# Which engine transposes blocks 10 to 23: the DMA crossbar or TensorE

## The chip, the cores and the metric

The kernel runs on one core of a Trainium2 chip. The metric is the device time of one execution in microseconds; for the kernel before there are three runs, and their median counts.

## The reference

Attention with a sliding window and four sink positions, for 4 batches of 8 heads, 768 positions and head size 64, followed by a normalised MLP with a residual:

```python
scores = scale * np.matmul(q, k.transpose(0, 1, 3, 2))
keep = (pos[None, :] < 4) | ((rel >= 0) & (rel < 128))      # rel = row - column
a = softmax(np.where(keep, scores, -1e9))
attn = a @ v                                                # x: heads side by side, (4, 768, 512)
xn = (x - mean) / sqrt(var + 1e-6) * g_ln
out = x + np.maximum(xn @ w_ch1, 0.0) @ w_ch2               # w_ch1 512x2048, w_ch2 2048x512
```

## The kernel before

The rows are cut into 24 blocks of 128 (6 for each batch). Block t needs its own q, k and v and the k and v of block t - 1, and from the third block of a batch on also the four sink positions. For each block the kernel does the following.

- *Load* (L265 to L285): q, k and v come from HBM as bf16 into `qkn` and `vn`, by DMAs that POOL issues. `qkn` lives in the ring `ld` of four buffers.
- *Transpose of q and k* into `qkT` (ring `qk`, five buffers). Blocks 0 to 9 use TensorE: eight 128x128 transposes at L348 into one PSUM bank `pt`, and a copy at L354 from there, by ACT or DVE. Blocks 10 to 23 use one DMA transpose at L370, issued by SP, from `qkn` straight to `qkT`. Either way the transpose gives the `ld` buffer back.
- *Scores* at L407 (`ps`), sink scores at L414 (`pk`, with `ks`, the sink keys of the batch copied at L455 from the batch's first `qkT`), exponentials on ACT at L436 and L483 (`e`, `es`), the mask on DVE at L445.
- *Values* at L497, L502 and L505 (`po`), normalisation on DVE at L515 and L518 (`xt`), the centred and scaled row `xc` at L530, and the variance at L539 and L540.
- *Transpose of `xc`* into `xnt`, the MLP's input for a group of four blocks. Blocks 0 to 9: four TensorE transposes at L561 into a bank `px`, and a copy at L576 by ACT or DVE. Blocks 10 to 23: one DMA transpose at L567, issued by SP.

The MLP works on six groups of four blocks. `m1` has 16 quanta of four 128x512 matmuls (L599, `ph`), each followed by a ReLU on ACT or DVE (L612 or L610, `h`); `m2` has 16 quanta of four (L625, `pc`), and after every fourth DVE adds the residual, scaled with `rsg` (L637, `ot`), and SP stores a block (L644). That is 192 quanta. `rsg` is made on POOL at L550.

The order on every engine is written when the program is built. `Planner` takes each piece of work as a task with estimated costs, the buffers that it takes and gives back, and a priority; it repeatedly takes the task that could start earliest by its estimates, so attention and MLP quanta are interleaved on TensorE. On the chip each engine works through its list in that order and waits where an input or a buffer is not there yet. The scores of block t from t = 5 on depend on quantum 8(t - 4) - 8 (the last loop of the kernel), which spreads them over the MLP. Four PSUM banks, the ring `pa`, serve `pt`, `px`, `po`, `pk`, `pv`, `ph` and `pc`; two double banks serve `ps`. In the first 24 us `warm` fills planned gaps of TensorE with matmuls that nobody reads (L184).

The two branches that test the set `DTR` are these:

```python
elif t in DTR:          # L363
    def dtr(e, s): ...  # one dma_start_transpose for all of q and k, on SP
...
if t in DTR:            # L563
    def dxt(e, *s2): ...  # one dma_start_transpose of xc, on SP
```

Of the kernel before, what the change touches and what calls it, by code (L numbers as in the profile page):

```python
# [129 lines left out]
def kernel(  # L130
# [22 lines left out]
    NT = B * RB  # L153
# [177 lines left out]
    def block(t):  # L331
# [27 lines left out]
        if split:  # L359
# [6 lines left out]
            d_t[t] = tq  # L366
        elif t in DTR:
            def dtr(e, s):
                qkT[t] = buf("qk", s, [128, 2, 4, 128], BF16, "qkT")
                nc.sync.dma_start_transpose(qkT[t].rearrange("p a h c -> p (a h) c"),  # L370
                                            qn[t].rearrange("p a h d -> p (a h d)"))
# [190 lines left out]

        if t in DTR:  # L563
            def dxt(e, *s2):
                if s2:
                    xnt[g] = buf("xn", s2[0], [128, NDM, 512], BF16, "xnt")
                nc.sync.dma_start_transpose(xnt[g][:, :, 128 * ti:128 * (ti + 1)], xc[t])  # L567
# [79 lines left out]

    SPLIT = set(range(8))
    SPLIT_S = set(range(4))
    DTR = set(range(10, NT))  # L650
    DTL = 1.5
    LAND = .9
    WARM_UNTIL = 24.0
# [62 lines left out]
```

## Time and profile before

| what | value |
|---|---|
| median of three runs | 231.85 us (231.32 to 232.07) |
| profiled execution: time | 232.07 us |
| profiled execution: span | 230.3 us |
| TensorE busy | 222.6 us, 97% |
| VectorE busy | 135.3 us, 59% |
| ScalarE busy | 106.6 us, 46% |
| GpSimd busy | 76.2 us, 33% |
| granted TensorE clock | 0.998 of full speed |
| `qkT<-qkn` DMA transposes | 14, landing after 7.6 us (median) |
| `xnt<-xc` DMA transposes | 14, landing after 3.4 us (median) |

The span runs from the first to the last instruction of the profiled execution; its time is 1.8 us more, for what lies around the span. In the profile PE is TensorE, PEld its weight loads, DVE VectorE, ACT ScalarE, POOL GpSimd and SP the queue engine; a tile `out<-in` names what is written and read, and L is the line of the kernel. The busy share of an engine is an average over stages; the chain of waits is followed back from the last instruction to what released each step. A matmul's length contains the depth of the pipeline, so lengths of neighbouring matmuls overlap, and their cost is the distance from one start to the next.

### The profile page before, as it was taken

How to read it: one execution, taken by the hardware profiler on the slowest of the kernel's cores; microseconds unless marked ns; L12 is line 12 of the kernel's file. 1: busy time of each engine (PE TensorE's matmuls, PEld its weight loads, DVE VectorE, ACT ScalarE, POOL GpSimd, SP SyncE). 2: the span in 40 equal slices, each digit the busy share in tenths (PEclk: the TensorE clock that was granted, in tenths of full speed). 3: DMA queues.
4: the chain of work that ended last, by engine and by line, in shares of the span. 5: the costliest groups of instructions: out<-in, count | busy, mean ns of one | idle time of the engine just before them, and what ended most of it. 6: DMA issues, size and time to landing. Idle time of an engine off the chain costs nothing.

```text
span 230.3 us, 4775 instructions
## 1 busy us (share of the span) xinstructions
PE 222.6 (97%) x1950; PEld 118.3 (51%) x1950; DVE 135.3 (59%) x376; ACT 106.6 (46%) x162; POOL 76.2 (33%) x92
## 2 busy tenths in 40 slices
PE   8999998999999999999999999999999999999993
PEld 7567543566555555444545544454554554444441
DVE  5775800399998959765567666845855755100121
ACT  2387266568456751156650356642067530276000
POOL 7993174988435780734041400001000001000000
PEclk9999999999999999999999999999999999999999
DMA  7999999999999999996959982023121022200112
GB/s 46 141 157 204 201 206 168 155 182 157 140 174 128 160 164 154 191 173 118 109 36 179 150 181 54 16 55 117 54 62 23 0 55 85 91 0 3 46 46 91
DMA packets 104983, 25.74 MB, mean 112 GB/s; under 512 B 97793, under 2 KB 101889, under 8 KB 104962
## 3 DMA queue, kind: packets, MB, share of 16 engines
q0 software_dynamic: 79104, 13.64, 80.9%
q1 hardware_dynamic: 25858, 11.80, 26.2%
q8 instruction: 15, 0.25, 0.4%
q14 instruction: 6, 0.05, 0.1%
HBM read 27.27 MB, written 6.29 MB: 146 GB/s over the span
## 4 chain that ended last, share of the span: by engine, by line
PE 77%; DMA 15%; POOL 5%; DVE 1%; issue 1%; ACT 0%; POOLq 0%
PE pc L625 36%; PE ph L599 28%; DMA qkn<-in_k_dram 7%; PE ps L407 4%; DMA w1s<-in_moe_w_ch_dram 4%; DMA qkT<-qkn 3%; PE po L502 2%; PE po L505 2%; POOL qkn L270 2%; POOL vn L278 2%; POOL qkn L275 2%; PE po L497 1%; PE pk L414 1%; PE pt L348 1%; PE px L561 1%
## 5 line engine op out<-in xcount | busy, mean ns | idle before, releaser
L625 PE MATMUL pc<-w2s,h 128*128 128x512 bf16 x384 | 88.9, 379 | 0.1
L599 PE MATMUL ph<-xnt,w1s 128*128 128x512 bf16 x384 | 88.1, 379 | 0.1
L612 ACT ACTIVATE h<-ph 128x512 bf16<-128x512 f32 x82 | 49.0, 597 | 61.3 <-PE ph L599 61.3
L599 PEld LDWEIGHTS <-w1s 128*128 128x128 bf16 x384 | 35.8, 98 | 39.8 <-issue 0.2
L625 PEld LDWEIGHTS <-h 128*128 128x128 bf16 x384 | 35.7, 98 | 39.2 <-DVE xt L518 0.2
L436 ACT ACTIVATE e<-ps 128x1024 bf16<-128x1024 f32 (+1 forms) x48 | 43.4, 952 | 9.2 <-PE ps L407 9.2
L637 DVE SCALAR_TENSOR_TENSOR ot<-pc,rsg,xt 128x512 f32<-128x512 f32 x24 | 18.0, 749 | 31.4 <-PE pc L625 30.9
L270 POOL DMA_DIRECT2D qkn<-in_q_dram x24 | 21.5, 896 | 42.3 <-DMA qkT<-qkn 36.2
L550 POOL TENSOR_TENSOR rsg<-ve,eps_half 128x4 f32<-128x4 f32 x6 | 6.4, 1066 | 70.5 <-DVE ve L548 70.5
L445 DVE TENSOR_TENSOR e<-e,mask_std 128x1024 bf16<-128x1024 bf16 x28 | 18.9, 685 | 10.2 <-ACT e L436 10.2
L275 POOL DMA_DIRECT2D qkn<-in_k_dram x24 | 21.5, 896 | 2.9 <-DMA w2s<-in_moe_w_ch_dram 1.5
L278 POOL DMA_DIRECT2D vn<-in_v_dram x24 | 21.6, 903 | 1.6 <-DMA qkn<-in_q_dram 1.0
L518 DVE SCALAR_TENSOR_TENSOR xt<-po,rc 128x256 bf16<-128x256 f32 x48 | 20.4, 425 | 1.7
L530 DVE SCALAR_TENSOR_TENSOR xc<-xt,sums,gb 128x512 bf16<-128x512 bf16 x24 | 18.0, 752 | 0.8
L483 ACT ACTIVATE es<-pk 128x256 bf16<-128x256 f32 x16 | 6.1, 384 | 24.7 <-PE pk L414 24.6
L502 PE MATMUL po<-vn,e 128*128 128x65 bf16 x192 | 17.1, 193 | 0.0
L539 DVE BATCH_NORM_STATS2 st<-xt 128x6 f32<-128x512 bf16 x24 | 16.4, 684 | 0.0
L610 DVE TENSOR_SCALAR h<-ph 128x512 bf16<-128x512 f32 x14 | 9.6, 686 | 10.0 <-PE ph L599 9.9
L502 PEld LDWEIGHTS <-e 128*128 128x128 bf16 x192 | 14.1, 97 | 2.0
L407 PEld LDWEIGHTS <-qkT 64*128 64x128 bf16 x352 | 9.9, 94 | 10.1 <-issue 8.1
L505 PE MATMUL po<-vn,e 128*128 128x65 bf16 x160 | 14.9, 193 | 0.0
L407 PE MATMUL ps<-qkT 64*128 64x128 bf16 x352 | 14.7, 218 | 0.0
(69 smaller groups left out, 147.3 us busy)
## 6 DMA issues: line engine op xcount, KB each, us to landing
out_dram<-ot SPq DMA_DIRECT2D x24, 256.0 KB, 2.0
qkn<-in_q_dram POOLq DMA_DIRECT2D x24, 128.0 KB, 6.6
qkn<-in_k_dram POOLq DMA_DIRECT2D x24, 128.0 KB, 6.8
vn<-in_v_dram POOLq DMA_DIRECT2D x24, 128.0 KB, 7.2
w1s<-in_moe_w_ch_dram POOLq DMA_DIRECT2D x4, 512.0 KB, 10.7
w2s<-in_moe_w_ch_dram POOLq DMA_DIRECT2D x4, 512.0 KB, 17.9
qkT<-qkn SPq DMA_TRANSPOSE x14, 7.6
xnt<-xc SPq DMA_TRANSPOSE x14, 3.4
```

The source lines that it names most:

```text
L270: nc.gpsimd.dma_start(qn[t][:, 0], q[b, :, rows, :].rearrange("h p d -> p h d"))
L275: nc.gpsimd.dma_start(qn[t][:, 1], k[b, :, rows, :].rearrange("h p d -> p h d"))
L278: nc.gpsimd.dma_start(vn[:, t, :, 0:64], v[b, :, rows, :].rearrange("h p d -> p h d"))
L407: nc.tensor.matmul(ps[:, h2, hh, kb, :], lhsT=qkT[t - kb][rows, 1, hp, :], rhs=qkT[t][rows, 0, hp, :], start=(hh == 0 and kb == 0 and t no ...
L436: nc.scalar.activation(E[t, half][:, :, :, 0:nkb, :], P["ps", t, half][:, :, :, 0:nkb, :], AF.Exp, scale=scale)
L445: nc.vector.tensor_mul(ee[:, :, 0:w], ee[:, :, 0:w], m[:, 0:w].unsqueeze(1).to_broadcast([128, 4, w]))
L502: nc.tensor.matmul(po[:, hh, :], lhsT=ee[:, h % 2, hh // 2, 0, :], rhs=vn[:, t, h, :], start=(r < 2 and hh == 0), stop=(r == 0), skip_grou ...
L505: nc.tensor.matmul(po[:, hh, :], lhsT=ee[:, h % 2, hh // 2, 1, :], rhs=vn[:, t - 1, h, :], start=False, stop=True, skip_group_check=True)
L518: nc.vector.scalar_tensor_tensor(xt[t][:, 256 * half:256 * half + 256].rearrange("p (h d) -> p h d", h=4), in0=po[:, :, 0:64], scalar=1.0, ...
L599: nc.tensor.matmul(ph, lhsT=w1s[:, j, 128 * ht:128 * (ht + 1)], rhs=xnt[g][:, j, 0:n], start=(j == 0), stop=(j == NDM - 1))
L612: nc.scalar.activation(o, i, AF.Relu)
L625: nc.tensor.matmul(P["pc", t], lhsT=h1[g, ht][:, 128 * ti:128 * (ti + 1)], rhs=w2s[:, ht, :], start=(ht == 0), stop=(ht == NH1 - 1))
```

## The change

`DTR`, the set of blocks whose transposes go through the DMA crossbar, becomes empty. Blocks 10 to 23 then take the TensorE branches for both transposes: L348 with L354 in place of L370, and L561 with L576 in place of L567. The planner orders the tasks anew, with one bank of `pa` and one copy for each moved transpose. Lines keep their numbers.

```diff
     SPLIT = set(range(8))
     SPLIT_S = set(range(4))
-    DTR = set(range(10, NT))
+    DTR = set()
     DTL = 1.5
     LAND = .9
     WARM_UNTIL = 24.0
```

## The prediction

> **What bounds the kernel now.** I read the busy table and the 40 slices first, then the chain of waits, then PE's own waits and its rows in order of time.
>
> ```profile
> span 230.3 us, 4775 instructions
> PE 222.6 (97%) x1950; PEld 118.3 (51%) x1950; DVE 135.3 (59%) x376; ACT 106.6 (46%) x162; POOL 76.2 (33%) x92
> PE 77%; DMA 15%; POOL 5%; DVE 1%; issue 1%; ACT 0%; POOLq 0%
> ```
>
> PE is busy nearly everywhere and carries 77% of the chain. The DMA share of that chain looks like a target, but most of it is the loads of the opening; of the transfers that the change touches only `DMA qkT<-qkn`, 3%, stands in it. Whether PE can take more work without lengthening the end is a question of its idle time after the first moved block, which is about 57 us. The stretches (columns: PE, PEld, DVE, ACT, POOL busy, clock, DMA share, GB/s) answer it:
>
> ```profile
> 56.90:100.00 43.10, 42.99 (x392) 22.60 (x390) 36.62 (x103) 19.39 (x30) 23.65 (x27) 1.00 1.93 162
> 100.00:150.00 50.00, 49.57 (x417) 24.95 (x417) 32.58 (x88) 26.79 (x42) 9.15 (x10) 1.00 1.03 108
> 150.00:189.00 39.00, 39.00 (x354) 19.89 (x353) 24.63 (x62) 18.33 (x27) 1.01 (x1) 1.00 0.18 49
> 189.00:226.00 37.00, 37.00 (x180) 16.78 (x176) 7.17 (x16) 9.55 (x16) 1.01 (x1) 1.00 0.15 54
> ```
>
> Out of 169 us PE is idle for 0.11 + 0.43 = 0.54 us. PE's list of waits from 56 us to the end has a single entry:
>
> ```profile
> PE pk L414 <- DVE xt L518: 0.4, 1, 0.4
> ```
>
> In the chain that wait is the end of `108.83 7.75 DMA qkT<-qkn`, the two `ks` copies and one normalisation: PE's sink scores of block 18 stood behind a crossbar transpose that came late. That is all that the crossbar costs PE directly.
>
> A busy PE may still be a PE that waits, because matmul ends are modelled. So I take start to start. These are PE rows in order of time (start, length, line, tile):
>
> ```profile
> 53.36 0.61 PE L348 MATMUL pt<-ident,qkn 128*128 128x128 bf16 x8
> 53.81 1.03 PE L625 MATMUL pc<-w2s,h 128*128 128x512 bf16 x4
> ...
> 64.32 0.39 PE L561 MATMUL px<-ident,xc 128*128 128x128 bf16 x4
> 64.55 0.28 PE L497 MATMUL po<-vs,es 128*128 128x130 bf16 x2
> ...
> 76.07 3.63 PE L599 MATMUL ph<-xnt,w1s 128*128 128x512 bf16 x16
> 79.53 0.28 PE L497 MATMUL po<-vs,es 128*128 128x130 bf16 x2
> ...
> 212.37 13.98 PE L625 MATMUL pc<-w2s,h 128*128 128x512 bf16 x64
> ```
>
> Eight transposes of `qkn` cost 53.81 - 53.36 = 0.45 us, 56 ns each, though the groups give each a length of 220 ns: the lengths overlap. Four transposes of `xc` cost 64.55 - 64.32 = 0.23 us. A 512-wide matmul costs 3.46/16 = 0.216 us. PE is the bound from 40 us on, at its own pace, and anything added to it after that is added to the end.
>
> **What the Trainium skill says.** "TensorE: Matmul & The Clock Gate", section "Wait — 56ns, not 53.3ns?", gives a start-to-start of 55.6 ns for 128 columns and 215.7 ns for 512 at full clock; the trace agrees (56 and 216 ns). The same page, "Part 4: PE-mode transpose", gives about 390 ns in isolation and about 275 ns in a kernel for a 128x128 transpose, says that it ends in PSUM and needs a copy, and that transposes do not count as work for the clock gate. The trace has a length of 219 ns and the copy; the clock stays at 1.00 in the windows with transposes, which come in runs of 4 to 16 between matmuls. "Perfetto Trace Analysis", section "Identifying the Most-Contended Engine", warns that matmul busy is a poor measure since pipelined instructions overlap; hence I price by spacing. "VectorE: DVE Perf Modes", section "The three transpose paths", gives 1309 ns for a 128x128 block through the crossbar; here one `qkT` transfer of eight blocks lands after 7.6 us (median), about 0.95 us a block, and one `xnt` transfer of four after 3.4 us.
>
> **The change part by part.** `DTR` becomes empty, so blocks 10 to 23, 14 of them, leave both branches that test it.
>
> *Removed.* 14 `qkT<-qkn` and 14 `xnt<-xc` transposes go from SP's queue and from the DMA engines, and SP then issues `g_row` and the 24 stores alone. The issue of one takes 1.2 to 3.9 us of SP. Stores were queued between them in order; no wait for a free `ot` buffer stands in the list of waits, so earlier stores gain nothing. The DMA engines get rid of packets in a stretch that is full until about 100 us, which lets the loads land sooner. Value: the 0.43 us above at most.
>
> *Added to PE.* 14 x 8 transposes at L348 and 14 x 4 at L561: 168 more, and the built instruction order has just these 168 (with a weight load each). 14 x 0.45 + 14 x 0.225 = 6.3 + 3.15 = 9.45 us. Nothing covers them, by the idle time above. The weight loads hide as those of the present 80 and 40 do: their cost is inside the 56 ns.
>
> *Added to DVE and ACT.* Each moved transpose needs a copy from PSUM. The built order puts 8 of the 14 `qkT` copies on ACT and 6 on DVE, 8 of the `xnt` copies on ACT and 6 on DVE, and moves two `h` from ACT to DVE. ACT: 8 x 1.015 + 8 x 0.59 - 2 x 0.60 = 11.6 us. DVE has no row for a copy of 128x1024; the 128x512 one takes 0.42, so it lies between 0.42 and 0.84, and I take 0.7: 6 x 0.7 + 6 x 0.42 + 2 x 0.69 = 8.1 us. From 57 to 189 us, 142 us long with the added PE time, DVE would be busy 93.8 + 8.1 = 102 us (72%) and ACT 64.5 + 11.6 = 76 us (54%). Both have room on the whole, but DVE is 96% busy between 50 and 70 us and five transposes (blocks 10 to 14) fall between 60 and 80 us. There I followed the built order: between the third and the fourth `ot` of group 0, DVE has about 9.1 us of work by its rows (6.0 before) and PE 7.6 us. DVE's rows overlap by some 10%, so about 8.2 us against 7.6, and the fourth `ot` comes roughly half a microsecond to one later than PE would like. With four `pa` banks, and the `px` and `pt` copies on ACT, which is half idle there, I see a delay of some tenths on PE, not more.
>
> *Added waits.* PE now waits in order for loads that the SP queue waited for. Behind a waiting `pt` stand all matmuls. In the built order `pt` of block 10 comes right behind the `px` that ran at 60.15 us and block 11 after one `po` half. Their k loads were issued at 49.13 and 52.33 us and took 7.6 and 7.5 us: landed by 56.7 and 59.8 us. Block 12 would be read at about 63.7 us; its k load, issued at 55.62, took 8.2 us with the first crossbar transposes beside it, so it lands before 63.8. Later blocks have more slack: `ld` slots now come free at the PE transpose instead of the crossbar's, which ends the 36.2 us that POOL waited for `qkT<-qkn`. On POOL `rsg` stands behind loads that wait for `pt`; by the built order it is still ahead of its `ot` by more than 10 us.
>
> *Extra stalls.* The trace of before has no stretch with all of this, so both ends: at best the small gaps near 60 us (0.18, 0.26 and 0.13 us before three matmuls) go too, -0.5 us; at worst each of the 14 blocks holds PE for a quarter of a copy, 14 x 0.15 = +2 us. I take +0.3.
>
> *Sum.* 9.45 - 0.43 + 0.3 = 9.3 us. The profiled execution took 232.07 us (span 230.3 and 1.8 around it), which is the highest of the three runs, 0.2 above their median of 231.85. 232.07 + 9.3 = 241.4 in its terms, 231.85 + 9.3 = 241.2 for the median. I say 241.3.
>
> **The rivals.**
> 1. *PE time is all* (the above): 240.4 to 242.2 us, chance 0.80.
> 2. *Banks.* `pt` and `px` now share four banks with `ph`, `pc`, `po`, `pk` through all MLP quanta, and ACT copies `pt` behind two exponentials of 1.02 us. If PE waits 0.25 us a block, 3.5 us are added: 244.8; with less, 242.2 to 245. Against it: blocks 4 to 9 did the same between 40 and 60 us and PE lost under 1 us there. Chance 0.14.
> 3. *Crossbar traffic slows the matmuls* (ends on the other side). Place: the 498 matmuls of 512 columns between 57 and 190 us, whose operands come from SBUF while transposes write it. If each were 19 ns quicker without them (197 ns), 9.4 us would come back: 231.9, no change; beyond that faster. Against it: 216 ns with crossbar transposes in flight (76 us) and, after 212 us with none, (13.98 - 0.16)/64 = 216 ns, 0.16 being how much longer the last row is than its spacing. Chance 0.03.
> 4. *The crossbar waits are worth more than listed*: earlier landings also remove the gaps of 1 us before 40 us. They lie ahead of the first moved transpose, so this gives at best 239.5 to 240.4. Chance 0.03.
>
> **How the numbers follow.** Case 1 gives the time. The range goes from 240.0 to 243.5: case 1, the upper edge of case 4 and the lower part of case 2; outside are the rest of 2 (0.07), case 3 and part of 4. A difference of about 0.3% (0.7 us) is what a measurement of this kernel can tell from none. Slower: 0.97; within: 0.02; faster: 0.01.
>
> **What would show it.** In the profile after: `pt` x192 and `px` x96 at 56 ns spacing, no DMA transposes, PE still without idle time from 57 us to the end, span near 239.6; POOL's waits for `qkT<-qkn` gone, and no wait of `pk`. Wrong would be: PE rows with waits for `qkn` loads, for ACT or for DVE adding over 1.5 us (case 2), or 512-wide matmuls under 210 ns (case 3).

## The result, and the profile after

The changed kernel takes 241.42 us (median of four runs, 241.20 to 241.84), the kernel before 231.84 us (median of four). The ratio is 1.0419, with an interval of 1.0396 to 1.0441. The profiled execution took 241.47 us with a span of 239.7 us, against 230.3 before: 9.4 us more. Some executions of a kernel are slower than its others, and sometimes that is the profiled one: ratios leave out those more than 1.5% above the kernel's fastest, medians are over all, and traces are read for places and spacings, not for a kernel's time.

The head of the page after, the engines' line and the chain's shares by engine:

```profile
span 239.7 us, 5054 instructions
PE 232.8 (97%) x2118; PEld 128.6 (54%) x2118; DVE 142.5 (59%) x390; ACT 117.2 (49%) x176; POOL 76.0 (32%) x92
PE 76%; DMA 11%; DVE 6%; POOL 5%; issue 1%; POOLq 0%
```

PE has 168 matmuls more (1950 to 2118) and 10.2 us more of busy time, and is as full as before. DVE got 7.2 us and ACT 10.6 us more, and neither share moved by more than 3 points. These are the stretches after (columns: PE, PEld, DVE, ACT, POOL busy, clock, DMA share, GB/s); the last one starts and ends about ten microseconds later than its counterpart before:

```profile
56.90:100.00 43.10, 42.84 (x436) 24.43 (x433) 35.06 (x98) 24.19 (x36) 22.94 (x26) 1.00 1.40 115
100.00:150.00 50.00, 50.00 (x459) 27.04 (x457) 34.49 (x88) 25.91 (x38) 8.99 (x10) 1.00 0.46 57
150.00:199.00 49.00, 49.00 (x436) 25.80 (x436) 32.48 (x86) 24.29 (x37) 1.01 (x1) 1.00 0.07 26
199.00:236.00 37.00, 36.54 (x173) 16.45 (x170) 6.67 (x12) 10.14 (x17) 1.01 (x1) 1.00 0.12 45
```

PE idles 0.26 us between 57 and 199 us (the 0.46 in the last stretch lies behind the last matmul, which ends at 235.55). The 0.43 us in the stretch from 100 to 150 us is gone. PE's list of waits from 56 us on (who waited for what: us in total, times, longest) again has one entry, another one than before:

```profile
PE pt L348 <- DVE xt L518: 0.2, 1, 0.2
```

It is the second moved `pt`, and it shows why DVE's share of the chain went from 1% to 6%: between 47 and 61 us the chain now runs mostly through DVE's list, and it comes back to PE here:

```profile
60.46 0.61 PE L348 MATMUL pt<-ident,qkn 128*128 128x128 bf16 x8
61.01 0.19 PE L502 MATMUL po<-vn,e 128*128 128x65 bf16 x1
...
61.57 0.61 PE L348 MATMUL pt<-ident,qkn 128*128 128x128 bf16 x8 [0.15 <-DVE xt L518]
```

So PE and DVE are nearly level at that place, and PE idled 0.15 us for DVE there.

One block's share can be read from PE's rows in order of time (start, length, line, tile). This is the stretch from the scores of one block to those of the next in the kernel after:

```profile
77.37 0.62 PE L407 MATMUL ps<-qkT 64*128 64x128 bf16 x16
...
79.02 0.61 PE L348 MATMUL pt<-ident,qkn 128*128 128x128 bf16 x8
79.47 3.62 PE L599 MATMUL ph<-xnt,w1s 128*128 128x512 bf16 x16
...
86.23 0.39 PE L561 MATMUL px<-ident,xc 128*128 128x128 bf16 x4
86.55 0.62 PE L407 MATMUL ps<-qkT 64*128 64x128 bf16 x16
```

and this the same in the kernel before:

```profile
125.70 0.62 PE L407 MATMUL ps<-qkT 64*128 64x128 bf16 x16
...
134.20 0.62 PE L407 MATMUL ps<-qkT 64*128 64x128 bf16 x16
```

The distance from scores to scores was 134.20 - 125.70 = 8.50 us and is 86.55 - 77.37 = 9.18 us. The surplus of 0.68 us is one set of transposes, 0.45 for `pt` (79.47 - 79.02) and about 0.23 for `px`.

The waits of POOL for `qkT<-qkn` (36.2 us) did not vanish; they changed their name, since POOL issues a load only when a `ld` buffer is free:

```profile
POOL qkn L270 <- PE pt L348: 38.9, 9, 10.7
```

PE does not wait for those loads after 57 us, as its list of waits shows, and the median landing time of a k load fell from 6.8 to 5.7 us.

### The profile page after: what moved, and what is told of

Same layout as the page of the kernel before. It is cut to its first block, busy times and chain, and to the rows that moved or that the text cites. A ratio compares the mean times of both kernels' runs of the same rounds, so it can differ in the third digit from the quotient of the medians.

```text
span 239.7 us, 5054 instructions
## 1 busy us (share of the span) xinstructions
PE 232.8 (97%) x2118; PEld 128.6 (54%) x2118; DVE 142.5 (59%) x390; ACT 117.2 (49%) x176; POOL 76.0 (32%) x92
## 4 chain that ended last, share of the span: by engine, by line
PE 76%; DMA 11%; DVE 6%; POOL 5%; issue 1%; POOLq 0%
PE pc L625 32%; PE ph L599 29%; DMA qkn<-in_k_dram 7%; DMA w1s<-in_moe_w_ch_dram 4%; PE ps L407 4%; PE pt L348 3%; PE po L502 2%; PE px L561 2%; POOL qkn L270 2%; PE po L505 2%; POOL vn L278 1%; POOL qkn L275 1%; PE po L497 1%; DVE e L445 1%; PE pk L414 1%; DVE xt L518 1%
## 5 line engine op out<-in xcount | busy, mean ns | idle before, releaser
L625 PE MATMUL pc<-w2s,h 128*128 128x512 bf16 x384 | 90.4, 379 | 0.1
L599 PE MATMUL ph<-xnt,w1s 128*128 128x512 bf16 x384 | 89.2, 379 | 0.1
L612 ACT ACTIVATE h<-ph 128x512 bf16<-128x512 f32 x80 | 47.8, 597 | 42.3 <-PE ph L599 42.3
L625 PEld LDWEIGHTS <-h 128*128 128x128 bf16 x384 | 35.2, 98 | 36.8 <-DVE xt L518 0.4
L270 POOL DMA_DIRECT2D qkn<-in_q_dram x24 | 21.8, 906 | 43.9 <-PE pt L348 38.9
L576 ACT COPY xnt<-px 128x512 bf16<-128x512 bf16 x12 | 7.0, 585 | 36.0 <-PE px L561 36.0
L354 DVE COPY qkT<-pt 128x512 bf16<-128x512 bf16 (+1 forms) x14 | 7.4, 536 | 22.6 <-PE pt L348 22.5
L610 DVE TENSOR_SCALAR h<-ph 128x512 bf16<-128x512 f32 x16 | 11.0, 690 | 11.1 <-PE ph L599 11.0
L502 PE MATMUL po<-vn,e 128*128 128x65 bf16 x192 | 17.1, 193 | 0.0
L354 ACT COPY qkT<-pt 128x1024 bf16<-128x1024 bf16 (+1 forms) x18 | 14.6, 838 | 2.2 <-PE pt L348 2.2
L348 PE MATMUL pt<-ident,qkn 128*128 128x128 bf16 x192 | 14.9, 219 | 0.7 <-DMA qkn<-in_k_dram 0.5
```

Source lines behind the costliest of these rows:

```text
L270: nc.gpsimd.dma_start(qn[t][:, 0], q[b, :, rows, :].rearrange("h p d -> p h d"))
L348: nc.tensor.transpose(P["pt", t, a][:, aa, hp, :], qn[t][:, aa, 2 * hp:2 * hp + 2, :], ident)
L354: (nc.scalar.copy if e == "ACT" else nc.vector.tensor_copy)(qkT[t][:, sl], P["pt", t, a][:, sl])
L502: nc.tensor.matmul(po[:, hh, :], lhsT=ee[:, h % 2, hh // 2, 0, :], rhs=vn[:, t, h, :], start=(r < 2 and hh == 0), stop=(r == 0), skip_grou ...
L599: nc.tensor.matmul(ph, lhsT=w1s[:, j, 128 * ht:128 * (ht + 1)], rhs=xnt[g][:, j, 0:n], start=(j == 0), stop=(j == NDM - 1))
L612: nc.scalar.activation(o, i, AF.Relu)
```

## The experiments

Theory A (the prediction's first case): the slowdown is PE time alone, 56 ns for each of 168 transposes. Theory B (its second): a good part of it comes from banks, copies and in-order waits. Theory C (its third): crossbar traffic slows the matmuls, and its absence gives something back. Rival D, for the way back, is lateness of the crossbar.

### PE time without the transposes (e1, e9)

Twelve idle 128x128 matmuls per block, added to the kernel before, into the bank of the scores. In e1 they stand between the halves of the scores:

```diff
                 for half, s in zip(halves, slots):
                     ps = P["ps", t, half] = buf("ps", s, ...)
+                    if t in DTR and half == 1:
+                        for _ in range(12):
+                            nc.tensor.matmul(ps[:, 0, 0, 0, :], lhsT=ident, rhs=ident, start=True, stop=True, ...)
```

> The kernel before, with its crossbar transposes kept, and for blocks 10 to 23 twelve 128x128 matmuls more in the score task, into the PSUM bank that the scores then overwrite: the PE time of the moved transposes without their banks, copies and waits, and without taking the crossbar's traffic away. Theory A (the slowdown is PE time alone, 168 x 56 ns = 9.4 us on a PE that has no idle time): 231.8 + 9.4 = 241.2 us. Theory B (a good part comes from banks, copies and in-order waits of the PE path): under 239 us, with the missing part being what they cost. Theory C (crossbar traffic slows the matmuls or is late in a way that matters, so that taking it away gives something back): above 242 us, since here the PE time is added and nothing is given back.

Measured: 244.4 us, ratio 1.0543 (1.0491 to 1.0595), above what A gave and on C's side. Whether that is C depends on where the surplus lies. PE's rows of e1:

```profile
112.78 0.40 PE L410 MATMUL ps<-qkT 64*128 64x128 bf16 x8
113.10 0.84 PE L397 MATMUL ps<-ident 128*128 128x128 bf16 x12
113.88 0.40 PE L410 MATMUL ps<-qkT 64*128 64x128 bf16 x8
...
122.17 0.40 PE L410 MATMUL ps<-qkT 64*128 64x128 bf16 x8
```

Scores to scores is 122.17 - 112.78 = 9.39 us, that is 0.89 more than 8.50, where twelve matmuls at 56 ns make 0.67. The remaining 0.22 us is two changes between 64-row and 128-row matmuls: the twelve take 113.88 - 113.10 = 0.78 us to the next start and not 0.67, and the other 0.11 us lies at the change ahead of them. Fourteen times 0.22 is 3 us. The Trainium skill, "TensorEngine Tiling (Array Packing)", section "Key Properties", says that a change of the tiling mode drains TensorE, without a figure; this trace agrees that a change costs time and gives about 0.1 us for one. To test it, e9 moves the twelve ahead of all 64-row matmuls of the block, where a change stands anyway:

```diff
                     if half == halves[0]:
                         warm(...)
+                        for _ in range(12 if t in DTR else 0):
+                            nc.tensor.matmul(ps[:, 0, 0, 0, :], lhsT=ident, rhs=ident, start=True, stop=True, ...)
```

> As the first experiment (the kernel before with twelve 128x128 matmuls more in each score task of blocks 10 to 23), but the twelve stand ahead of all 64-row score matmuls of the block and not between their halves. The first experiment gave 244.4 us; its trace puts the surplus over 241.2 on two more changes between 128-row and 64-row matmuls in each block, about 0.1 us each, and on a wait of 1.1 us for a load of qkn around 40 us, ahead of the first change. If that reading holds, here the changes are not more than before and theory A gives 231.3 + 9.4 = 240.7 us within 0.5 (no wait around 40 us). If the PE time of idle matmuls costs more for another reason, it stays at 243 to 244.

Measured: 240.61 us, ratio 1.0388 (1.0352 to 1.0423). The rows:

```profile
120.99 0.83 PE L396 MATMUL ps<-ident 128*128 128x128 bf16 x12
121.76 0.62 PE L409 MATMUL ps<-qkT 64*128 64x128 bf16 x16
...
130.17 0.83 PE L396 MATMUL ps<-ident 128*128 128x128 bf16 x12
130.94 0.62 PE L409 MATMUL ps<-qkT 64*128 64x128 bf16 x16
```

130.94 - 121.76 = 9.18 us, the distance of the changed kernel. Matmuls that nobody reads, with the crossbar path kept whole, cost what the change costs within the two intervals (9.0 us by this ratio, 9.7 by that of the change). That is A: B and C are not needed. One part of the expectation missed: the profiled execution still had a load wait of 1.4 us around 40 us; it lies ahead of everything that was changed.

### Crossbar traffic beside the PE transposes (e2)

```diff
             cq = plan.add({"DVE": .70, "ACT": 1.0}, [tq], cp(None), ...)
+            if t >= 10:
+                def dead(e):
+                    nc.sync.dma_start_transpose(scrap..., qn[t]...)
+                plan.add({"SP": .5}, [tq], dead, (0, t, 0), land=2.0, lag=DTL, drop=[("ld", t)])
...
+        if t >= 10:
+            def dead_x(e):
+                nc.sync.dma_start_transpose(scrap_x, xc[t])
+            plan.add({"SP": .5}, [x], dead_x, (0, t, 8), land=1.0, lag=DTL, drop=[("xc", t)])
```

> The changed kernel with its PE transposes, and beside them the same 28 crossbar transposes as in the kernel before, into buffers that nobody reads; the order on PE, DVE and ACT is that of the changed kernel. The dead transposes hold the ld and xc buffers until they are done. Theory A: the traffic costs PE nothing, 241.4 us within 0.5. Theory C: traffic slows the matmuls, then more than 243 us, and the 512-wide matmuls stand more than 216 ns apart where the crossbar is busy. Theory B says nothing against 241.4, but loads that come later because ld buffers are held longer could add a wait of PE for qkn.

Measured: 241.08 us, ratio 1.0404 (1.0359 to 1.0450). The issues of its page show that the traffic is there (out<-in, queue, count, median us to landing):

```profile
scrap<-qkn SPq DMA_TRANSPOSE x14, 5.1
scrap_x<-xc SPq DMA_TRANSPOSE x14, 2.5
```

and PE's rows in order of time show that it changes nothing:

```profile
76.97 0.62 PE L415 MATMUL ps<-qkT 64*128 64x128 bf16 x16
...
79.06 3.62 PE L612 MATMUL ph<-xnt,w1s 128*128 128x512 bf16 x16
...
86.14 0.62 PE L415 MATMUL ps<-qkT 64*128 64x128 bf16 x16
```

Scores to scores is 9.17 us, and sixteen 512-wide matmuls have a length of 3.62 us, both as without the traffic. Over all neighbouring 512-wide matmuls of this trace between 57 and 190 us, the median from start to start is 216 ns with one of these transfers in flight and 216 ns with none. Theory C is out.

### One transpose at a time, and half of the blocks (e3, e4, e5)

e3 moves q and k alone, e4 `xc` alone; e5 moves both for blocks 10 to 16:

```diff
 # e3
-        if t in DTR:          # the branch of xc
+        if t >= 10:
-    DTR = set(range(10, NT))
+    DTR = set()
 # e4
-        if t in DTR:          # the branch of xc
+        if t < 0:
 # e5
-    DTR = set(range(10, NT))
+    DTR = set(range(17, NT))
```

> Only the transposes of q and k of blocks 10 to 23 go to PE; those of xc stay on the crossbar. Theory A: 112 x 56 ns = 6.3 us, less up to 0.4 for the wait of pk behind a late qkT: 231.8 + 5.9 to 6.3 = 237.7 to 238.1 us. Theory B: the bank of pt and its copy of 1 us are the costly part, so this has nearly all of the slowdown: 239 to 241 us.

> Only the transposes of xc of blocks 10 to 23 go to PE; those of q and k stay on the crossbar. Theory A: 56 x 56 ns = 3.15 us: 231.8 + 3.15 = 235.0 us, within 0.4; the wait of pk for a late qkT may stay. Theory B: px is in order behind the normalisation and LayerNorm chain on DVE, so PE waits for xc: above 236 us if that is where the stalls are, or under 234 if the cost sits with pt.

> Blocks 10 to 16 go to PE for both transposes, 17 to 23 stay on the crossbar. Theory A: half of the PE time, 7 x 0.675 = 4.7 us, and the wait of pk may go or stay: 236.1 to 236.5 us. Theory B: the stalls lie between 60 and 70 us, where DVE is 96% busy and five transposes fall together, so the early half carries more than half: above 237 us.

| run | median us | ratio (interval) | PE time by A | more than before, by the ratio |
|---|---|---|---|---|
| e3, q and k alone | 237.56 | 1.0263 (1.0219 to 1.0306) | 6.3 us | 6.1 us |
| e4, `xc` alone | 234.45 | 1.0125 (1.0083 to 1.0167) | 3.15 us | 2.9 us |
| e5, blocks 10 to 16 | 236.47 | 1.0221 (1.0182 to 1.0260) | 4.7 us | 5.1 us |
| both, all blocks | 241.42 | 1.0419 (1.0396 to 1.0441) | 9.45 us | 9.7 us |

The last column is the ratio less one, times 231.84 for the last row and the median of before in their series (231.42, 231.42, 231.1) for the others. In each row A's PE time lies within the interval of the ratio. e3 and e4 came out 0.14 and 0.15 us under the ranges that were given in us, which had been counted from 231.8 us, where the kernel before took 231.42 in their series. The two parts add up to the whole within the intervals, and the early half of the blocks, with the full stretch of DVE, costs no more than its share within 1 us.

### All copies on DVE (e6)

```diff
-            cq = plan.add({"DVE": .70, "ACT": 1.0}, [tq], cp(None), ...)
+            cq = plan.add({"DVE": .70} if t >= 10 else {"DVE": .70, "ACT": 1.0}, [tq], cp(None), ...)
...
-        d_xn[t] = plan.add({"DVE": .43, "ACT": .59}, ...)
+        d_xn[t] = plan.add({"DVE": .43} if t >= 10 else {"DVE": .43, "ACT": .59}, ...)
```

> The changed kernel, but the PSUM copies of blocks 10 to 23 may go to DVE alone: ten copies that ACT made (10 x 1.0 and 12 x 0.59 us less on ACT, of which the moved blocks' share is 8 and 8) go to DVE, about 8 x 0.69 + 8 x 0.42 = 8.9 us more there. Theory A: copies lie beside PE work, DVE goes from 72% to 78% of the stretch: 241.4 us within 0.6. Theory B: banks wait for copies behind DVE's queue between 57 and 100 us, where DVE has little room: 243 to 246 us.

Measured: 241.73 us, ratio 1.0438 (1.0396 to 1.0481), the same as the changed kernel. All 14 moved copies of `qkT` (128x1024) now stand on DVE, and 20 of the 24 copies of `xnt` (128x512), the 14 moved ones among them:

```profile
L354 DVE COPY qkT<-pt 128x1024 bf16<-128x1024 bf16 x14 | 9.5, 686 | 7.4 <-PE pt L348 7.4
L576 DVE COPY xnt<-px 128x512 bf16<-128x512 bf16 x20 | 8.4, 419 | 3.1 <-PE px L561 3.0
```

Had PE waited on banks behind copies, a fuller DVE would have shown it. With e9, where no bank and no copy is added, theory B is out for this kernel, but for some tenths of a microsecond near 60 us.

### The way back: more on the crossbar (e7, e8, e10, e11)

If PE time is the price, moving more transposes off PE should gain 56 ns each. Four kernels tried it, all edits of the kernel before:

```diff
 # e7
+    DTR = set(range(8, NT))
 # e8: the branch of xc
+        if t >= 4:
 # e10: the branch of xc
+        if t >= 8:
 # e11
+    DTR = set(range(8, NT))
+    DTL = 6.0
```

> The other way: blocks 8 and 9 too leave PE for the crossbar. Theory A: 2 x 0.675 = 1.35 us of PE time goes: 230.5 us. Rival D (the crossbar is late where loads keep the DMA engines full, as around 50 us, and PE then waits for qkT at the scores of blocks 8 and 9): 231.5 to 234 us, with waits of ps or pk for DMA qkT in PE's list.

> The other way for xc alone: blocks 4 to 9 too transpose xc on the crossbar, q and k stay as before. Theory A: 6 x 4 x 56 ns = 1.35 us of PE time goes, and six PSUM copies with it: 230.5 us. Rival D: the crossbar's transfers land late between 45 and 75 us, where loads fill the DMA engines, and the first ph of a group waits for xnt: 231.5 us or more, with a wait of ph for xnt.

> The other way in its smallest step: only the xc of blocks 8 and 9 leave PE for the crossbar, both in a group that the MLP needs only at 100 us. Theory A: 8 x 56 ns = 0.45 us of PE time goes: 230.8 us, which is hardly more than what can be measured. Rival D (crossbar transfers, or the SP queue behind them, late where loads fill the DMA engines): slower than the kernel before, 231.5 to 233 us, with a wait of PE for qkT or xnt in its trace.

> Blocks 8 and 9 on the crossbar for both transposes, and the planner told of a landing time 4.5 us longer for every crossbar transpose (DTL 6.0 in place of 1.5), which is nearer to the 7.6 us that the trace shows for qkT, so that it puts scores and first MLP quanta later. Theory A with the lateness planned for: 1.35 us less PE time: 230.0 us. Rival D: the DMA engines are full until 60 us, so the transfers of blocks 8 and 9 and the loads behind them are late by more than the plan knows and POOL's loads wait longer for ld: 232 to 237 us.

e10, the smallest step, gave 231.11 us against 231.56, ratio 0.9988 (0.9958 to 1.0018): no difference that can be told, and what A gives (0.45 us, a ratio of 0.998) lies in the interval. e7's six executions spread from 232.75 to 237.56 us (median 236.83, above what D gave); the ratio of 1.0119 (1.0045 to 1.0193) rests on two of them, and no place is read from its trace. It is no gain. e8 and e11 were far slower: 246.46 us, ratio 1.0625 (1.0571 to 1.0680), and 242.46 us, ratio 1.0498 (1.0450 to 1.0547). Their lists of PE's waits name the place, first e8, then e11:

```profile
PE ph L599 <- DMA xnt<-xc: 13.9, 1, 13.9
```

```profile
PE ph L599 <- DMA xnt<-xc: 8.3, 1, 8.3
```

In e8 the MLP's second group (blocks 4 to 7) waits for the `xnt` of block 7. These are the pieces of the chain for the `xc` of block 7 (first line) and for its transfer (last line), with SP's rows between them:

```profile
64.20 0.75 DVE xc L530
67.88 1.23 SPq L370 DMA_TRANSPOSE qkT<-qkn  x1
69.21 4.23 SPq L567 DMA_TRANSPOSE xnt<-xc  x2
70.49 9.31 DMA xnt<-xc
```

The `xc` was there at 64.95 us, but its transpose, the second `xnt` in SP's last row, was issued at 70.49, 5.5 us later. In the order that the planner wrote for SP, two transposes stand ahead of it: a `qkT`, before which SP waited 3.0 us for a k load, and the `xnt` of block 8, which belongs to the next group. Then the transfer took 9.31 us, at a time when loads and other crossbar transposes keep the DMA engines 90% busy or more; the same transfer takes 2.4 us late in the kernel, when the loads are done. In the kernel before, these blocks' transposes are on PE, and the copy is there about a microsecond after them.

In e11 the wait is that of the third group for the `xnt` of block 11 (DVE's row for its `xc`, then SP's rows for the `xnt` of blocks 12 and 11):

```profile
89.47 0.75 DVE L530 SCALAR_TENSOR_TENSOR xc<-xt,sums,gb 128x512 bf16<-128x512 bf16 x1
97.73 1.21 SPq L567 DMA_TRANSPOSE xnt<-xc  x1
100.11 1.27 SPq L567 DMA_TRANSPOSE xnt<-xc  x1
```

Here the `xc` was there at 90.22 us and lay for 9.9 us: ahead of its transpose SP has three stores, each of which waits for its `ot`, the `xnt` of block 10, which was late in the same way, and that of block 12, which waits for an `xc` made at 97.70. The transfer itself took 6.94 us. Issued at 90.22 it would have landed at about 97.2 us (an estimate from these numbers), and PE stopped at 98.9. So the longer planned landing did not help, and it may have done the harm (not tested): each `xnt` is planned behind the landing of the group's previous one, and block 12 begins a new group.

For e8 and e11, D was put as lateness of the transfers where loads fill the DMA engines. That is one part of what happened. The order on SP's queue is the other, and in e11, which at 242.46 us lies above D's range, the larger one. No kernel with that order put right was run, so what the crossbar would give below block 10 stays open. How many blocks may go to it depends on how full the DMA engines are, on what stands ahead in SP's list, and on how soon the MLP needs the group. No version beat the kernel before by more than can be measured.

## Why the prediction was right

It said 241.3 us; the median is 241.42. Step by step:

- *PE has no idle time to absorb work after 57 us.* Held. e9 shows it best: idle matmuls alone, with nothing else changed, gave 240.61 us. It is tight near 61 us, where DVE is nearly level with PE.
- *168 transposes at 56 ns, 9.45 us.* Held: 0.68 us from scores to scores per block, e3 and e4 as parts. The row's mean length of 219 ns would have given 37 us.
- *The wait of `pk`, -0.43 us.* The price held: the wait is gone, and PE is full between 100 and 150 us. The reading was off in one point. The `pk` that waited at 117.74 us is that of block 15 (block 18 begins a batch and has no sink scores). It waited for DVE's normalisation of block 14, and DVE had stood 3.53 us before the `ks` copies until the `qkT` of block 18 landed (`116.61 0.39 DVE L455 COPY ks<-qkT 64x128 bf16<-64x128 bf16 x2 [3.53 <-DMA qkT<-qkn]`). A late transfer for one block held up the work of others through DVE's order.
- *Copies beside the path.* Held: DVE's copy of 128x1024, taken as 0.7 us between 0.42 and 0.84, is 0.688; e6 could load DVE with all of them at no cost that can be measured. The busy times rose less than the sums (7.2 against 8.1 us on DVE, 10.6 against 11.6 on ACT).
- *Stalls of +0.3 us.* About right, in the place that was named; as a pick between -0.5 and +2 it owes something to luck. Start to start, PE's gaps beyond its own pace near 60 us add up to 1.0 us in the kernel after (0.27, 0.16, 0.11, 0.32 and 0.15) and 0.56 before: +0.45. 9.45 - 0.43 + 0.45 = 9.5, against 9.4 between the spans and 9.6 between the medians. The two small terms cancel, so the 9.45 carries the result.
- *The end of POOL's wait for `qkT<-qkn`.* Half wrong, without a price: it became a wait of 38.9 us for `pt`. A likely reason, not tested, is that a `pt` needs a `qkT` buffer, which the scores give back, so that they set the pace of the loads either way.
- *Rivals.* Banks (B) failed in e6 and e9, crossbar traffic (C) in e2. The waits for loads around 40 us (the fourth case) come and go between profiled executions: 0.46 us in the kernel after, and with the crossbar path kept 0.69 (before), 0.46 (e10) and 1.8 us (e9).

## What to carry to other kernels

When one engine is full from some point to the end, the price of moving work onto it is count times spacing, start to start in the trace; the length of a pipelined row overstates it (here fourfold) and the landing time of the transfer that it replaces is no measure of the gain. Before moving work the other way, ask who needs the transfer first, what stands ahead of it in the queue that issues it, and how full the DMA engines are at that time: 1.35 us of PE time freed for `xc` cost 15 us in e8. And a control that adds idle work has a place too: put it where it adds no change of mode.

## What was not expected of the hardware

A change between 64-row and 128-row matmuls cost PE about 0.1 us (e1: 0.22 us for two, one in each direction). And PE was slow for a while after it had stood still. These are the stretches of e8 around its wait (columns as above):

```profile
66.00:80.00 14.00, 0.14 (x2) 0.14 (x2) 5.23 (x18) 0.00 (x0) 8.48 (x10) 0.51 2.05 153
80.00:94.00 14.00, 13.67 (x112) 6.64 (x114) 6.76 (x17) 8.61 (x13) 2.63 (x3) 0.88 1.28 111
94.00:108.00 14.00, 13.80 (x121) 7.13 (x123) 9.85 (x28) 5.20 (x8) 4.40 (x5) 1.00 1.06 113
```

The granted clock was 0.51 while PE waited and 0.88 in the 14 us after; the first sixteen score matmuls took 0.97 us there in the chain and not 0.55. The Trainium skill, "TensorE: Matmul & The Clock Gate", section "What's actually happening", says that the clock is halved after an idle window of about 3.4 us and comes back after as much work. The trace agrees on the half and on the way back: a mean of 0.88 over 14 us is half speed for 0.12 x 14 / 0.5 = 3.4 us. It does not show a full idle window ahead of the drop: by the mean of 0.51 the clock was halved less than half a microsecond after PE stopped at 66.03 us, though PE had also stood for 1.9 us shortly before. A wait of 14 us thus cost more than 14 us.
